# Attention and mixture of experts on one core: the gate's logits from fp16 halves in three products

## The chip, the core and the metric

The kernel runs on one core of a Trainium2 chip. Its time is device time in microseconds (us). Engines: PE (TensorE, matmuls and transposes; its weight loads are listed as PEld), DVE (VectorE), ACT (ScalarE), POOL (GpSimd), and SP, which only issues DMAs here. PE writes to PSUM, a small memory of 8 banks that DVE and ACT read. Each engine runs its instructions in the order of the program and waits where an operand is not there yet.

## The reference

Three stages: attention in a causal window of 128 keys, a mixture of experts with one expert per token, and a dense layer with the maximum of three products. The change touches the gate's logits, between the first and the second.

```python
def _attn_ref(q, k, v):                       # q, k, v: [4, 8, 576, 64]
    ...
    return np.matmul(attn, v)

def _moe_ref(x, modality_id, w_gate, modality_bias, w1, w2):   # x: [2304, 512], 8 experts
    logits = x @ w_gate + modality_bias[modality_id]
    e_idx = np.argmax(logits, axis=1)
    ...                                        # probs = softmax(logits)
    gate_w = probs[np.arange(N), e_idx]
    for e in range(E):
        mask = e_idx == e
        h = np.maximum(x[mask] @ w1[e], 0.0)
        out[mask] = gate_w[mask, None] * (h @ w2[e])

def _moe2_ref(x, w1, w2, w3, w_out):
    h = np.maximum(np.maximum(x @ w1, x @ w2), x @ w3)
    return h @ w_out
```

## The kernel before

Tokens are taken in tiles of 128 rows of one batch entry b: tiles t = 0 to 3 are full, t = 4 has 64 rows. A group is (b, t, g) with g = 0 or 1 for four of the eight heads; t = 4 holds all heads in one group. `run` (L485) walks over 36 groups and issues, in group n, work of several groups: the product with V of group n-3 (`pv`, L390, on PE), the softmax of group n (four score reductions L348 on DVE, four exponentials L357 on ACT), the scores of group n+1 or n+2 (`qk`, L335), the transposes of group n-1's exponentials (L376) with their split into an fp16 high half (ACT, L382) and low half (DVE, L387), and the normalisation (L432 to L436 on DVE). Where a product has to be more precise than fp16, both operands are held as a high and a low fp16 half and three products are added: high by high, high by low, low by high (PASSES, L916).

When both head groups of a tile are done, its rows are turned by `xt` (L453): four transposes on PE into a PSUM tile (L458), and a copy to SBUF in fp32 on ACT (L460). `logits` (L463) is issued one group later: four fp32 matmuls of 128x8 against the gate weights wg (L468). `logit_out` (L478) adds the modality's bias on DVE (L479) and writes to L, from which `Route` finds each token's expert. The last full tile (t = 3) and the half tile (t = 4) of a batch entry come in the same group; there the first one's logits are issued directly behind its transposes.

The first groups run alone (from the start to about 97 us). Then `att.mixed` is set, and the attention's steps are woven between the matmuls of the experts' first batches (`slot`, L978; products L994 and L1015, weights split by L957 on ACT and L966 on DVE). In this mode the logits are issued at the start of a group, right behind `qk`, and their output follows at once. Which step stands where is fixed when the program is built. Four PSUM tiles of the pool psM are shared by transposes, turned rows, logits and the experts' products; one is taken again when its last reader is done. After the attention (about 262 us) DVE converts the third stage's weights (L1110 to L1121).

`RouterConsts.bias` (L172) runs in the first groups as small pieces, one at each call of `fill`, between the reductions of the softmax.

Of the kernel before, what the change touches and what calls it, by code (L numbers as in the profile page):

```python
# [7 lines left out]
F32 = mybir.dt.float32  # L8
F16 = mybir.dt.float16
BF16 = mybir.dt.bfloat16  # L10
I32 = mybir.dt.int32
ACTF = mybir.ActivationFunctionType
ALU = mybir.AluOpType
# [4 lines left out]
E, FF, F2 = 8, 1024, 768  # L18
WIN = 128
HALF = NT // 2  # L20
NTB = 5
# [10 lines left out]
KD, KF, K2 = DM // 128, FF // 128, F2 // 128  # L32
SV = 256.0
SX = 64.0
SW = 64.0
# [6 lines left out]
NG = 2  # L42
WAIT = 3
PLACES = 2


@with_exitstack
def windowed_attention_moe_kernel(
# [16 lines left out]
    nc = tc.nc  # L65
    PSUM = bass.MemoryType.PSUM
    const = ctx.enter_context(tc.tile_pool(name="const", bufs=1))
# [16 lines left out]
    iota_e = const.tile([128, 2 * NTB, E], F32, name="iota_e")  # L84
    ones_r = const.tile([1, 128], F16, name="ones_r")
    wg = const.tile([128, KD, E], F32, name="wg")
    mbt = const.tile([128, B, NTB, E], F32, name="mbt")
    parts = const.tile([128, 2 * NTB, 6], F16, name="parts")

# [21 lines left out]
    class Bias:  # L111


        def __init__(self, pool, pf, bias, nq, widths):
            self.bias, self.nq = bias, nq
            tot = sum(widths)
            self.rf = pf
            if nq < 128:
                self.rf = pool.tile([128, 1], F32, name=f"c_rf{nq}")
                nc.vector.tensor_copy(self.rf[0:nq], pf[0:nq])  # L120
                nc.vector.tensor_scalar(self.rf[nq:], pf[nq:], float(-nq), None, ALU.add)
            self.ci = pool.tile([128, tot], I32, name=f"c_ci{nq}")
            o = 0
            for w, base in zip(widths, (-WIN, 0)):
                nc.gpsimd.iota(
                    self.ci[:, o:o + w], base=base,
                    pattern=[[1, w]], channel_multiplier=0,
                )
                o += w
            self.rel = pool.tile([128, tot], F32, name=f"c_rel{nq}")  # L130
            self.t = pool.tile([128, tot], F32, name=f"c_t{nq}")
# [23 lines left out]
    class RouterConsts:  # L155
# [16 lines left out]
        def bias(self):  # L172
            pool = self.pool
            mr = pool.tile([36, 128], F32, name="c_mr")
            nc.vector.tensor_copy(
                mr, self.mi.rearrange("r (p two) -> r p two", two=2)[:, :, 0]
            )
            yield 4
            ps = psM.tile([128, 512], F32, name="m", tag="m")
            nc.tensor.transpose(ps[:, 0:36], mr, ident[0:36, 0:36])  # L180
            yield 4
            mf = pool.tile([128, B, NTB], F32, name="c_mf")
            nc.vector.tensor_copy(
                mf[:, :, 0:4], ps[:, 0:16].rearrange("p (b r) -> p b r", r=4)
            )
            nc.vector.tensor_copy(mf[:, :, 4], ps[:, 32:36])
            yield
            mf = mf.rearrange("p b t -> p (b t)")
            mn = pool.tile([128, B * NTB], F32, name="c_mn")
            nc.vector.tensor_scalar(mn, mf, -1.0, 1.0, ALU.mult, ALU.add)  # L190
            yield
            mt = pool.tile([128, B * NTB, E], F32, name="c_mt")
            sh = [128, B * NTB, E]
            mbo = mbt.rearrange("p b t e -> p (b t) e")
            nc.vector.tensor_tensor(
                out=mbo, in0=mn.unsqueeze(2).to_broadcast(sh),
                in1=self.mb[:, 0:1, :].to_broadcast(sh), op=ALU.mult,
            )
            yield
            nc.vector.tensor_tensor(  # L200
                out=mt, in0=mf.unsqueeze(2).to_broadcast(sh),
                in1=self.mb[:, 1:2, :].to_broadcast(sh), op=ALU.mult,
            )
            yield
            nc.vector.tensor_tensor(out=mbo, in0=mbo, in1=mt, op=ALU.add)
# [12 lines left out]
    L = [rt.tile([128, 2 * NTB, E], F32, name=f"L{h}") for h in range(2)]  # L218
# [33 lines left out]
    class Attention:  # L252
# [200 lines left out]
        def xt(self, t, x):  # L453
            kd = KD if t < 4 else KD // 2
            ps = psM.tile([128, KD, 128], F32, name="m", tag="m")
            xf = x.rearrange("p a b c -> p (a b c)")
            for kk in range(kd):
                nc.tensor.transpose(ps[:, kk, :], xf[:, 128 * kk:128 * kk + 128], ident)  # L458
            xt = self.p.tile([128, KD, 128], F32, name="xt", tag="xt", bufs=1)
            nc.scalar.activation(out=xt[:, 0:kd], in_=ps[:, 0:kd], func=ACTF.Copy)  # L460
            return xt

        def logits(self, b, t, xt):  # L463
            ps = psM.tile([128, 512], F32, name="m", tag="m")
            m, kd = (128, KD) if t < 4 else (64, KD // 2)
            for kk in range(KD):
                u, ku = divmod(kk, kd)
                nc.tensor.matmul(  # L468
                    out=ps[0:m, 0:E], lhsT=xt[:, ku, m * u:m * u + m], rhs=wg[:, kk, :],
                    start=(kk == 0), stop=(kk == KD - 1),  # L470
                )
            self.outs.append((b, t, m, ps))

        def logits_out(self):
# [2 lines left out]

        def logit_out(self, b, t, m, ps):  # L478
            nc.vector.scalar_tensor_tensor(  # L479
                out=L[b // 2][0:m, NTB * (b % 2) + t, :], in0=ps[0:m, 0:E], scalar=1.0 / SX,  # L480
                in1=mbt[0:m, b, t, :], op0=ALU.mult, op1=ALU.add,
            )
            self.got.add((b, t))
# [379 lines left out]
    class Gather:  # L863
# [42 lines left out]
        def send(self):  # L906
            for i in range(len(self.out)):
# [4 lines left out]
                    in_=xc[0:o.shape[3]].rearrange("p a c -> p (a c)"),  # L912
                )
                self.sent += 1

    PASSES = ((0, 0), (0, 1), (1, 0))  # L916

    class Weights:

# [58 lines left out]
    def slot(pool, wst, w0, xT, yT, d, cap):  # L978
# [9 lines left out]
        for m in range(KF):  # L988
# [3 lines left out]
            for kk in range(KD):  # L992
                for wl, xl in PASSES:
                    nc.tensor.matmul(  # L994
# [12 lines left out]
        for dm in range(KD):  # L1007
# [3 lines left out]
            for f in range(KF):  # L1011
                if f in (2, 4, 6):
                    yield 6 * cap / 2370, 0.6 if f == 4 and cap > 256 else 0
                for wl, xl in PASSES:
                    nc.tensor.matmul(  # L1015
# [128 lines left out]
    def moe2(pool, items, w, hmt, n2=C2, both=False, **kw):  # L1144
# [5 lines left out]
        def product(run, yT, c, m, i):  # L1150
            ps = psM.tile([128, 512], F32, name="m", tag="m")[:, 0:n2]
            n = 0
            for kk in range(KD):
                for wl, xl in PASSES:
                    nc.tensor.matmul(  # L1155
# [35 lines left out]
        def outer(x, yT, c, idxs, gates):  # L1191
            w.convert(w.n)
            hm = hms[:, x % 2]
            for u in range(n2 // 128):
# [3 lines left out]
                for f in range(K2):  # L1198
                    for wl, xl in PASSES:
                        nc.tensor.matmul(  # L1200
# [64 lines left out]
    class Batch:  # L1265
# [30 lines left out]
        def turn(self, wait=WAIT):  # L1296
# [7 lines left out]
            if not self.todo and not self.age and not self.done:  # L1304
                self.done = True
                if self.u % 2:
                    fill.add(self.r.late())
            for _ in range(PLACES):
                if self.age and self.age[0] >= wait:
# [210 lines left out]
```

## Time and profile before

| what | value |
|---|---|
| median of three runs | 695.49 us (693.38 to 697.06) |
| profiled execution | 695.69 us, span 693.9 us |
| PE busy | 644.1 us (93% of the span) |
| DVE busy | 351.8 us (51%) |
| ACT busy | 346.3 us (50%) |
| POOL busy | 222.5 us (32%) |
| granted clock of PE, mean | 0.979 |

The span runs from the first to the last instruction; the profiled execution's time is 1.8 us longer. Busy shares are means over stages with different limits, so the views by stretch tell more than the page's first section. A row of the timeline gives the start, the time from the start to the end of the last of its instructions, the engine, the line, and in square brackets the idle time ahead of it with what ended it. The end of a matmul is modelled and matmuls overlap, so the cost of small matmuls is read from starts.

### The profile page before, as it was taken

To read this page: it belongs to the slowest core of one execution; us is meant where nothing else is said; L and a number is where in the kernel's file an instruction comes from. 1 tells how busy PE (TensorE), PEld (TensorE's weight loads), DVE (VectorE), ACT (ScalarE), POOL (GpSimd) and SP (SyncE) were. 2 spreads that over 40 slices of the span, in tenths; PEclk is the share of its full clock that TensorE was granted. 3 is DMA by queue.
4 is the path that set the end of the run, shared out by engine and by line. 5 is a ranking of instruction groups with operands and counts; after the bars stand their busy time and mean duration, and the time that the engine had idled before them with its cause. 6 is when DMAs were issued, how large, how long until landed. Compare 5 with 4: busy or idle time off the path is not lost.

```text
span 693.9 us, 12894 instructions
## 1 busy us (share of the span) xinstructions
PE 644.1 (93%) x4787; PEld 401.9 (58%) x4787; DVE 351.8 (51%) x1083; ACT 346.3 (50%) x660; POOL 222.5 (32%) x232
## 2 busy tenths in 40 slices
PE   6899879999898989688899999999999999999993
PEld 4687756566665658354455564444447766656641
DVE  5977853875457656799971233062224455201100
ACT  5898876877777646645552211354647211111110
POOL 2111214524323213556662311482424111121121
PEclk9999988999999999899999999999999999999998
DMA  9655755345522237636833403344230000000011
GB/s 192 108 123 136 198 137 140 92 124 166 152 63 73 80 115 238 218 125 209 212 91 76 92 22 122 110 132 121 92 112 13 1 0 1 1 31 17 0 47 49
DMA packets 120800, 69.95 MB, mean 101 GB/s; under 512 B 68872, under 2 KB 115484, under 8 KB 120732
## 3 DMA queue, kind: packets, MB, share of 16 engines
q1 hardware_dynamic: 116992, 59.06, 32.0%
q0 software_dynamic: 3040, 9.96, 4.4%
q8 instruction: 40, 0.66, 0.4%
q14 instruction: 28, 0.23, 0.1%
q10 hardware_dynamic: 700, 0.04, 0.1%
HBM read 57.19 MB, written 9.44 MB: 96 GB/s over the span
## 4 chain that ended last, share of the span: by engine, by line
PE 71%; DVE 15%; ACT 7%; issue 3%; DMA 3%; POOL 0%; ACTq 0%; POOLq 0%; DVEq 0%
PE m L1155 22%; PE m L1015 12%; PE m L994 11%; PE m L1200 10%; PE s L335 4%; DVE b L1115 3%; PE m L376 3%; PE m L468 2%; PE bank L406 2%; PE m L283 2%; DMA st<-in_moe_w_dram 2%; DVE e L348 2%; DVE b L1121 1%; DVE b L1110 1%; ACT eh L382 1%
## 5 line engine op out<-in xcount | busy, mean ns | idle before, releaser
L1155 PEld LDWEIGHTS <-g 128*128 128x128 f16 x1296 | 128.1, 99 | 100.2 <-issue 12.7
L1155 PE MATMUL m<-yT,g 128*128 128x384 f16 x648 | 111.6, 336 | 11.9 <-ACT hx L1162 4.3
L1155 PE MATMUL m<-yh,g 128*128 128x384 f16 x648 | 105.7, 326 | 0.0
L966 DVE SCALAR_TENSOR_TENSOR wt<-st,wt 128x1024 f16<-128x1024 f32 x48 | 61.6, 1286 | 84.1 <-ACT wt L957 84.1
L1015 PE MATMUL m<-ht,wt 128*128 128x496 f16 (+3 forms) x576 | 101.9, 331 | 1.6 <-DVE wt L966 0.9
L1164 DVE SCALAR_TENSOR_TENSOR hx<-m,hx 128x384 f32<-128x384 f32 x72 | 39.8, 554 | 118.5 <-PE m L1155 117.9
L994 PEld LDWEIGHTS <-wt 128*128 128x128 f16 x576 | 54.6, 98 | 45.1 <-issue 3.2
L986 POOL TENSOR_TENSOR ht<-hf,ht 128x496 f16<-128x496 f32 (+3 forms) x48 | 50.1, 1049 | 86.7 <-ACT ht L985 78.5
L1015 PEld LDWEIGHTS <-wt 128*128 128x128 f16 x576 | 53.8, 98 | 39.3 <-DVE wt L966 1.1
L357 ACT ACTIVATE e<-e,nm 128x256 f32<-128x256 f32 (+2 forms) x144 | 59.8, 472 | 29.1 <-DVE nm L348 27.5
L984 ACT ACTIVATE hf<-m 128x496 f32<-128x496 f32 (+3 forms) x72 | 35.7, 496 | 59.0 <-PE m L1015 36.8
L994 PE MATMUL m<-xT,wt 128*128 128x496 f16 (+2 forms) x288 | 57.7, 341 | 3.1 <-ACT wt L957 1.6
L348 DVE CUSTOM_DVE_ANT_0 e<-s,bias 128x256 f32<-128x256 f32 (+1 forms) x128 | 46.0, 381 | 17.4 <-PE s L335 8.6
L957 ACT ACTIVATE wt<-st 128x1024 f16<-128x1024 f32 x48 | 50.0, 1045 | 4.3 <-DMA st<-in_moe_w_dram 4.2
L994 PE MATMUL m<-xh,wt 128*128 128x496 f16 (+1 forms) x288 | 51.1, 330 | 0.0
L387 DVE TENSOR_TENSOR el<-m,eh 128x512 f16<-128x512 f32 x64 | 42.4, 682 | 11.6 <-ACT eh L382 11.5
L335 PE MATMUL s<-kT,qT 64*128 64x256 f32 (+2 forms) x320 | 42.6, 384 | 3.3 <-DVE nm L348 2.2
L1186 POOL TENSOR_TENSOR xh<-hx,xh 128x384 f16<-128x384 f32 x18 | 16.4, 913 | 89.8 <-ACT xh L1185 89.8
L311 POOL TENSOR_TENSOR vl<-rawv,vh 128x512 f16<-128x512 f32 (+1 forms) x20 | 22.9, 1146 | 68.7 <-ACT vh L304 68.7
L1185 ACT ACTIVATE xh<-hx 128x384 f16<-128x384 f32 x18 | 9.4, 523 | 71.1 <-DVE hx L1164 67.1
L1206 ACT ACTIVATE ob<-m,gate 128x512 f32<-128x512 f32 x18 | 12.4, 687 | 55.0 <-PE m L1200 49.6
L382 ACT ACTIVATE eh<-m 128x512 f16<-128x512 f32 x64 | 34.8, 586 | 7.1 <-PE m L376 6.6
(184 smaller groups left out, 976.5 us busy)
## 6 DMA issues: line engine op xcount, KB each, us to landing
st<-in_moe_w_dram SPq DMA_DIRECT2D x66, 512.0 KB, 4.1
rawk<-in_k_dram SPq DMA_DIRECT2D x16, 256.0 KB, 3.3
rawq<-in_q_dram SPq DMA_DIRECT2D x16, 256.0 KB, 4.1
rawv<-in_v_dram SPq DMA_DIRECT2D x16, 256.0 KB
xs<-x SPq DMA_DIRECT2D x16, 256.0 KB, 2.1
st<-in_moe_w_out_dram SPq DMA_DIRECT2D x6, 512.0 KB, 6.3
rawk<-in_k_dram SPq DMA_DIRECT2D x4, 128.0 KB, 3.4
rawq<-in_q_dram SPq DMA_DIRECT2D x4, 128.0 KB, 4.9
```

The costliest lines, as they stand in the source:

```text
L335: nc.tensor.matmul(out=out[u][rows, x // 2, c0:c1], lhsT=self.qT[b, t][r, i, 0:n], rhs=self.kT[b][r, i, k0 + c0:k0 + c1], start=True, stop ...
L348: nc.vector.tensor_tensor_reduce(out=e[:, x, c0:c1], in0=s[x % 2][:, x // 2, c0:c1], in1=bias[:, x, c0:c1], scale=-0.125, scalar=3.0e38, o ...
L357: nc.scalar.activation(out=e[:, x, c0:c1], in_=e[:, x, c0:c1], func=ACTF.Exp, scale=-1.0, bias=nm[:, x:x + 1],)
L382: nc.scalar.activation(out=b, in_=a, func=ACTF.Copy)
L387: nc.vector.tensor_tensor(out=o, in0=a, in1=b, op=ALU.subtract)
L957: nc.scalar.activation(out=wt[:, 0], in_=st, func=ACTF.Copy, scale=SW)
L966: nc.vector.scalar_tensor_tensor(out=wt[:, 1], in0=st.rearrange("p (a b) -> p a b", a=a), scalar=SW, in1=wt[:, 0], op0=ALU.mult, op1=ALU.s ...
L986: nc.gpsimd.tensor_tensor(out=lo, in0=hf, in1=hi[1], op=ALU.subtract)
L994: nc.tensor.matmul(out=ps, lhsT=wt[:, wl, kk, o:o + 128], rhs=xT[:, xl, kk, bass.ds(d[0], cap)], start=(n == 0), stop=(n == 3 * KD - 1),)
L1015: nc.tensor.matmul(out=ps, lhsT=wt[:, wl, f, :], rhs=hs[f][:, xl], start=(n == 0), stop=(n == 3 * KF - 1),)
L1155: nc.tensor.matmul(out=ps, lhsT=w.g[:, wl, i, m, kk, :], rhs=yT[:, xl, kk, c:c + n2], start=(n == 0), stop=(n == 3 * KD - 1),)
L1200: nc.tensor.matmul(out=ps, lhsT=hm[:, xl, f, 128 * u:128 * u + 128], rhs=w.wo[:, wl, f, :], start=(n == 0), stop=(n == 3 * K2 - 1),)
```

## The change

The turned rows leave PSUM as two fp16 halves: ACT copies the high one, DVE subtracts it from PSUM to get the low one. The tile xt has two buffers instead of one. The gate weights, scaled by SW = 64, are split once into a high and a low half (wgs), in two new pieces of `RouterConsts.bias`. The logits become three fp16 matmuls for each of the four parts of the row, twelve in all, and the output divides by SW too.

```diff
+PASSES = ((0, 0), (0, 1), (1, 0))
...
+    wgs = const.tile([128, KD, 2, E], F16, name="wgs")
...
+            yield
+            nc.vector.tensor_scalar(wgs[:, :, 0], wg, SW, None, ALU.mult)
+            yield
+            nc.vector.scalar_tensor_tensor(
+                out=wgs[:, :, 1], in0=wg, scalar=SW, in1=wgs[:, :, 0],
+                op0=ALU.mult, op1=ALU.subtract,
+            )
             yield 4
...
-            xt = self.p.tile([128, KD, 128], F32, name="xt", tag="xt", bufs=1)
-            nc.scalar.activation(out=xt[:, 0:kd], in_=ps[:, 0:kd], func=ACTF.Copy)
+            xt = self.p.tile([128, 2, KD, 128], F16, name="xt", tag="xt", bufs=2)
+            nc.scalar.activation(out=xt[:, 0, 0:kd], in_=ps[:, 0:kd], func=ACTF.Copy)
+            nc.vector.tensor_tensor(
+                out=xt[:, 1, 0:kd], in0=ps[:, 0:kd], in1=xt[:, 0, 0:kd], op=ALU.subtract
+            )
...
-                nc.tensor.matmul(
-                    out=ps[0:m, 0:E], lhsT=xt[:, ku, m * u:m * u + m], rhs=wg[:, kk, :],
-                    start=(kk == 0), stop=(kk == KD - 1),
-                )
+                for i, (wl, xl) in enumerate(PASSES):
+                    nc.tensor.matmul(
+                        out=ps[0:m, 0:E], lhsT=xt[:, xl, ku, m * u:m * u + m],
+                        rhs=wgs[:, kk, wl, :],
+                        start=(kk == i == 0), stop=(kk == KD - 1 and i == 2),
+                    )
...
-                out=L[b // 2][0:m, NTB * (b % 2) + t, :], in0=ps[0:m, 0:E], scalar=1.0 / SX,
+                out=L[b // 2][0:m, NTB * (b % 2) + t, :], in0=ps[0:m, 0:E], scalar=1.0 / (SX * SW),
```

## Rows read from the trace of the kernel before

**Rows 1.** Stretches: length, then busy PE, PEld, DVE, ACT, POOL; clock, DMA.
```profile
20.00:34.00 14.00, 11.45 (x101) 8.14 (x100) 13.60 (x57) 12.14 (x27) 2.38 (x4) 1.00 0.54 103
...
34.00:97.00 63.00, 57.65 (x741) 49.61 (x742) 45.44 (x216) 52.94 (x120) 13.45 (x19) 0.97 0.63 157
104.00:262.00 158.00, 150.86 (x1427) 99.61 (x1427) 95.67 (x350) 110.45 (x210) 51.69 (x51) 0.99 0.39 111
262.00:360.00 98.00, 82.50 (x565) 53.14 (x565) 86.90 (x151) 51.70 (x98) 57.26 (x49) 0.93 0.62 191
```

**Rows 2.** Chain of waits, 34 to 97 us: start, length, engine, tile, line.
```profile
36.48 0.99 PE m L468 x8
...
95.08 0.99 PE m L468 x8
```

**Rows 3.** Line L468: durations least, median, greatest; starts; forms.
```profile
L468 PE MATMUL m<-wg,xt x160: 172/256/277, 36.4 to 261.8; 128*128 128x8 f32 x128, 128*64 128x8 f32 x32
```

**Rows 4.** Timeline of PE around a full tile's logits and a half one's.
```profile
157.40 1.06 PE L468 MATMUL m<-wg,xt 128*128 128x8 f32 x8
158.31 0.19 PE L406 MATMUL bank<-vh,eh 128*128 128x65 f16 x1
...
159.00 0.19 PE L406 MATMUL bank<-vh,el 128*128 128x65 f16 x1
...
61.27 0.63 PE L468 MATMUL m<-wg,xt 128*64 128x8 f32 x8
61.83 0.87 PE L376 MATMUL m<-ident,e 128*128 128x128 f32 x6
```

**Rows 5.** Timeline of PE, the routing's small products.
```profile
67.58 0.24 PE L662 MATMUL bank<-r_oh,ones 128*128 128x32 bf16 x4
67.68 0.28 PE L666 MATMUL bank<-r_gt,ones 128*128 128x40 bf16 x5
```

**Rows 6.** Lines L387 and L898, the subtraction of an fp16 half from PSUM.
```profile
L387 DVE TENSOR_TENSOR el<-m,eh x64: 667/681/692, 18.6 to 246.6; 128x512 f16<-128x512 f32 x60, 64x512 f16<-64x512 f32 x4
...
L898 DVE TENSOR_TENSOR xT<-m,xT x10: 416/681/692, 98.2 to 184.7; 128x512 f16<-128x512 f32 x8, 128x448 f16<-128x448 f32 x1, 128x256 f16<-128x256 f32 x1
```

**Rows 7.** Timeline around the turned rows copied at 43.18 us.
```profile
41.76 0.35 DVE L348 CUSTOM_DVE_ANT_0 e<-s,biast 128x192 f32<-128x192 f32 x1
...
43.18 0.59 ACT L460 ACTIVATE xt<-m 128x512 f32<-128x512 f32 x1
...
43.32 0.16 DVE L432 TENSOR_SCALAR rd<-bank 128x4 f32<-128x4 f32 x1 [0.65 <-PE bank L406]
...
44.22 1.28 DVE L387 TENSOR_TENSOR el<-m,eh 128x512 f16<-128x512 f32 x2
...
45.49 1.09 PE L376 MATMUL m<-ident,e 128*128 128x128 f32 x8 [0.58 <-ACT kT L297]
```

**Rows 8.** Timeline around the turned rows copied at 71.12 us.
```profile
70.39 0.40 DVE L348 CUSTOM_DVE_ANT_0 e<-s,bias 128x256 f32<-128x256 f32 x1
...
71.12 0.59 ACT L460 ACTIVATE xt<-m 128x512 f32<-128x512 f32 x1
...
73.18 0.16 DVE L432 TENSOR_SCALAR rd<-bank 128x4 f32<-128x4 f32 x1 [0.88 <-PE bank L406]
...
78.22 0.16 PE L786 MATMUL bank<-r_e,ones_r 1*128 1x1 f16 x1 [0.93 <-DVE rd L432]
```

**Rows 9.** Timeline of the woven stretch: one copy, and two logit outputs.
```profile
138.43 0.58 ACT L460 ACTIVATE xt<-m 128x512 f32<-128x512 f32 x1
...
141.95 0.17 DVE L479 SCALAR_TENSOR_TENSOR L<-m,mbt 128x8 f32<-128x8 f32 x1 [3.54 <-PE m L468]
...
248.85 0.17 DVE L479 SCALAR_TENSOR_TENSOR L<-m,mbt 128x8 f32<-128x8 f32 x1 [0.40 <-PE m L468]
```

**Rows 10.** Timeline around a batch entry's last full tile, near 190 us.
```profile
190.15 0.69 DVE L387 TENSOR_TENSOR el<-m,eh 128x512 f16<-128x512 f32 x1 [1.69 <-ACT eh L382]
...
190.66 1.06 PE L468 MATMUL m<-wg,xt 128*128 128x8 f32 x8 [0.93 <-ACT xt L460]
```

More of the change, by code (lines that the diff above doesn't have):

```diff
@@ L914, in send @@
                 self.sent += 1
-    PASSES = ((0, 0), (0, 1), (1, 0))
     class Weights:
```

## The prediction

> **What bounds the kernel now.** I read the stretches first. From 104 to 262 us, where MoE products are woven into the attention, PE is busy 150.86 of 158 us and DVE 95.67: PE is the bound and DVE has room. From 34 to 97 us, where attention runs alone, PE is busy 57.65 of 63 us, ACT 52.94 and DVE 45.44: three engines take turns, each waiting for another. From 262 to 360 us DVE is busy 86.90 of 98 us with work that the change does not touch [rows 1]. The order of instructions on every engine is fixed in the program, so time won or lost before 262 us moves all that follows by the same amount; I count only there. The chain of waits says the same of the first stretch: of its eight logit tiles, five are on the chain, from the one at 36.48 to the one at 95.08 [rows 2]. For the other three something else ends later.
>
> **What is removed.** A logit tile is four fp32 products, recorded as eight matmuls; there are 16 full tiles and 4 half ones [rows 3]. A full one holds PE from its start at 157.40 to the next work at 158.31, 0.91 us; a half one from 61.27 to 61.83, 0.56 us [rows 4]. The change puts twelve fp16 matmuls of 8 columns there. No row shows these, so I bound them: 24 fp16 matmuls with 128x128 weights and 65 columns start between 158.31 and 159.00, 30 ns apart [rows 4]; four with 16-bit weights and 8 to 32 columns start between 67.58 and 67.68, 25 ns apart [rows 5]. Twelve cost 0.30 to 0.36 us; I take 0.33, since 8 columns are nearest to the second row. PE saves 0.58 us in a full tile and 0.23 in a half one: 16 x 0.58 + 4 x 0.23 = 10.2 us if all of it lay on the path.
>
> The Trainium skill, page "FP8 and Floating Point Precision", section "TensorE Precision Notes", speaks against so large a saving: it counts true fp32 as four passes through the array, so that four fp32 products are 16 passes against twelve now. By that a full tile would still take 12/16 of its time. The rows show 25 to 30 ns for one 16-bit matmul and 114 ns (0.91/8) for one of the fp32 records, so here a pass of fp32 is not the price of a small fp16 matmul; but the rule is kept as a rival.
>
> **What is added.** DVE subtracts the fp16 half from PSUM, once per tile. The same operation on 128x512 takes 0.68 us (L387) and on 128x256 0.42 us (L898) [rows 6]: 16 x 0.68 + 4 x 0.42 = 12.6 us of DVE. ACT's copy keeps its shape and place; as fp16 output I cost it as before. The second buffer of the turned rows gives nothing: no row shows a copy that waits for the logits before it. The two conversions of the gate weights fall where DVE is busy 13.60 of 14 us [rows 1]; at 0.16 us for a tiny DVE operation [rows 7] that is +0.3.
>
> What matters is where the subtraction stands. DVE runs in program order. In the first stretch the subtraction is issued behind group n's work and ahead of the four score reductions of group n+1, and it waits for ACT's copy, which waits for PE's transposes. Three of these reductions now run early, while DVE would otherwise wait for the product with V. Take the tile at 43.18. ACT's copy ends at 43.77, the subtraction at 44.49; the three reductions that now run from 41.76 follow it (0.28 us apart) to 45.32. L432, now at 43.32, comes at 45.32, and the two L387, 0.9 us behind it and now at 44.22, come at 46.2. These release the PSUM that PE's next transposes need: the second half of what starts at 45.49 waits until 46.9 instead of about 46.0, and so does all behind it [rows 7]. Loss +1.1, and the 0.58 that PE saved is waited away. At 71.12 the same happens: the copy ends at 71.71, the subtraction at 72.4, 1.9 us of DVE work begun at 70.39 goes behind it, and L432 moves from 73.18 to about 74.3; PE waits for DVE there already (0.93 us at 78.22) [rows 8]. Loss +1.2. The other six tiles of the stretch I worked the same way; where DVE's wait for PE is over 2 us, the shift vanishes: +0.2, 0, +0.3 (full and half tile together), +0.5 and -0.6 (there the whole saving arrives). The subtraction also releases the PSUM of the transposes, later than ACT did, and the next transposes of K wait for that; this is in these numbers. Sum of the first stretch +2.7, bounds -2.9 (all five tiles on the chain save 0.58 and nothing waits) and +9.7 (seven full tiles each pay 0.59 + 0.68 and the half one 0.80).
>
> In the second stretch DVE sits idle 3.54 us ahead of the logit output at 141.95, because it waits for PE's logits. ACT's copy at 138.43 ends at 139.0, so the subtraction ends at 139.7, before the logits start at about 140.9: it is hidden there [rows 9]. Five full tiles are like that: 5 x 0.58 = -2.9. The three half tiles save 3 x 0.23 = -0.7. One tile (output at 248.85) has only 0.40 us of that idle time, and routing work ahead of the subtraction on DVE [rows 9]: +0.2. At the last full tile of a batch the logits are issued right behind the transposes and wait already, 0.93 us at 190.66; DVE is in L387 until 190.84, so the subtraction ends at 191.52 and the rest of the twelve at 191.8 instead of 191.57 [rows 10]. Three such tiles: +0.3, +0.1, +0.1. Behind the subtraction on DVE is the low half of a MoE weight, up to 2.6 us later; it is made two weight tiles ahead, and PE is hardly idle in this stretch, so I cost that at nothing (if that lead were gone, some 1 us a time). Sum -2.9; bounds -5.9 (all nine full tiles save the whole 0.58) and 0 (each saving is waited away).
>
> **Sum.** +0.3 + 2.7 - 2.9 = +0.1 us. The profiled execution took 695.69 us; its span is 693.9, and the 1.8 around it stay. 695.69 + 0.1 = 695.8; it lies 0.2 above the median of the runs, so I forecast 695.6.
>
> **Rivals.** *Faster*: the first stretch has slack that my step by step shift overstates; then the five tiles on the chain give 0.58 each. -2.9 - 2.9 + 0.3 = -5.5, 690 us. For it: DVE has 17.6 us of idle time there [rows 1]. Against: that idle time lies ahead of L432, and the two places worked above have 0.65 and 0.88 us of it, less than copy and subtraction together, 1.27.
> *Slower*: the wait of DVE for ACT's copy is paid in full by every tile of the first stretch, since DVE, PE and ACT each wait for the other in a ring. +9.7 - 2.9 + 0.3 = +7.1, 702.6 us. It decides wherever the idle time ahead of L432 is under 1.27 us and the late PSUM release reaches PE. For it: the two places. Against: the places with over 2 us of slack.
> *The products cost more*, a mechanism of their own: a tile takes 0.91 x 12/16 = 0.68 instead of 0.33. Five tiles lose 0.35, one of the first stretch too, three half tiles 0.09: +2.4, 698 us. It is the fp32 rule named above; the rows of 25 to 30 ns speak against it.
>
> **Chances.** Forecast 0.45, faster 0.28, slower 0.23, dear products 0.04. The forecast's own range is 692 to 699. For eight times in ten I reach into both sides: 689.5 to 701. About 0.5% (3.5 us, 692.0 to 699.0) is what a measurement of this kernel can tell from no change. Faster by more: 0.28 and a little of the forecast's edge, 0.30. Slower by more: 0.23 and an edge, 0.25. Within: 0.45.
>
> **What would show it.** After the change: the logit matmuls 25 to 30 ns apart; the subtraction 0.68 us, with DVE idle ahead of it for ACT's copy; in the first stretch L432 and L387 later against the group's start, and PE waiting for L387 or for the subtraction; in the second stretch the wait of the logit output shorter by some 0.6, PE's busy time 5 to 6 us less, and its end (262 us) within 2 us of where it is. I am wrong if the stretch 34 to 97 gets shorter (then DVE's order did not matter), if PE waits for MoE weights from DVE, or if the granted clock falls at new places.

## The result, and the profile after

The changed kernel takes 700.04 us (median, 698.55 to 703.26) against 695.08 us before (693.38 to 697.06) in the same comparison: a ratio of 1.008, 95% interval 1.006 to 1.010. It is slower by 5 us. That lies inside the range (689.5 to 701.0), above the forecast's own range (692 to 699), 4.4 us above the forecast and on the side that had a chance of 0.25. The profiled execution of after has a span of 699.2 us, 5.3 us over that of before.

The stretches of after, cut as in [rows 1] (length, then busy PE, PEld, DVE, ACT, POOL; clock, DMA):

```profile
20.00:34.00 14.00, 11.85 (x99) 8.73 (x98) 12.48 (x51) 11.75 (x25) 2.39 (x4) 0.92 0.49 97
34.00:97.00 63.00, 54.18 (x714) 44.30 (x714) 46.93 (x213) 50.63 (x112) 12.36 (x18) 0.93 0.60 146
104.00:262.00 158.00, 147.21 (x1445) 93.30 (x1445) 106.00 (x367) 112.45 (x211) 51.62 (x50) 0.98 0.39 108
262.00:360.00 98.00, 82.90 (x578) 53.87 (x579) 83.16 (x148) 52.21 (x99) 53.66 (x46) 0.91 0.61 188
```

From 34 to 97 us PE is busy 3.5 us less than in [rows 1] with 27 matmuls fewer: less work was done in the same time, and the mean granted clock fell from 0.97 to 0.93. From 104 to 262 us PE is busy 3.7 us less and DVE 10.3 us more.

The logit products and the subtraction are what the steps said. Line L481 (L468 before) and the timeline of PE:

```profile
L481 PE MATMUL m<-wgs,xt x240: 166/166/217, 38.7 to 267.3; 128*128 128x8 f16 x96, 128*64 128x8 f16 x24
...
38.73 0.46 PE L481 MATMUL m<-wgs,xt 128*128 128x8 f16 x12
...
39.04 1.08 PE L385 MATMUL m<-ident,e 128*128 128x128 f32 x8
```

The next work starts 0.31 us behind the first of the twelve (0.33 forecast; 0.91 before [rows 4]). What surrounds them is not. Here is the tile that the prediction worked through [rows 7], now copied at 44.91 us (start, length, engine, line, tile; in brackets the idle time before it and what ended it):

```profile
44.91 0.58 ACT L469 ACTIVATE xt<-m 128x512 f16<-128x512 f32 x1
44.93 0.48 PE L344 MATMUL s<-kT,qT 64*128 64x128 f32 x2
...
45.53 0.69 DVE L470 TENSOR_TENSOR xt<-m,xt 128x512 f16<-128x512 f32 x1 [1.97 <-ACT xt L469]
...
46.14 0.35 DVE L357 CUSTOM_DVE_ANT_0 e<-s,biast 128x192 f32<-128x192 f32 x1
...
46.92 0.68 PE L344 MATMUL s<-kT,qT 64*128 64x128 f32 x6 [1.51 <-DVE nm L357]
```

DVE stands still for 1.97 us until ACT has copied, subtracts, and only then makes the score reductions (L357). PE stops 1.51 us in the middle of the next score products: their PSUM tile has three buffers, and the readers that free one are those reductions. This link, from the subtraction to PE by way of the scores, was not in the prediction. DVE's own order came out as worked: L441 starts 2.06 us behind the start of the copy (46.97), where the prediction had 2.14. The chain of waits of after, 34 to 97 us, runs straight through it:

```profile
43.96 1.06 ACT eh L391 x2
45.02 0.49 ACT xt L469
45.53 0.69 DVE xt L470
```

DVE's wait for the copy recurs at nearly every tile. Waits of 34 to 97 us (total us, times, longest): first three rows of after, then the row of before that they replace.

```profile
DVE xt L470 <- ACT xt L469: 8.5, 7, 2.0
...
DVE rd L441 <- PE bank L415: 2.6, 2, 1.4
...
PE s L344 <- DVE nm L357: 1.7, 2, 1.5
```
```profile
DVE rd L432 <- PE bank L406: 8.3, 7, 2.2
```

DVE's idle time ahead of L432 (now L441) shrank from 8.3 to 2.6 us: it was the slack that should have hidden the subtraction, and 8.5 us of waiting for the copy took its place. What this costs PE is counted further below.

The last full tile of a batch entry, where the logits are issued right behind the transposes (before: [rows 10]):

```profile
190.56 1.38 PE L1006 MATMUL m<-xT,wt 128*128 128x480 f16 x6
...
193.33 0.18 PE L481 MATMUL m<-wgs,xt 128*128 128x8 f16 x1 [0.95 <-ACT xt L469]
...
193.57 0.68 DVE L470 TENSOR_TENSOR xt<-m,xt 128x512 f16<-128x512 f32 x1
...
194.31 0.43 PE L481 MATMUL m<-wgs,xt 128*128 128x8 f16 x11 [0.81 <-DVE xt L470]
...
194.86 2.00 PE L1006 MATMUL m<-xT,wt 128*128 128x480 f16 x6
...
197.50 2.07 PE L1006 MATMUL m<-xT,wt 128*128 128x480 f16 x6
...
195.00:200.00 5.00, 5.00 (x21) 2.69 (x20) 1.56 (x2) 3.37 (x8) 1.10 (x1) 0.66 0.25 74
```

The first product waits 0.95 us for the copy as before, the eleven others 0.81 us for the subtraction. Behind this the granted clock of 195 to 200 us is 0.66, a time spent mostly at the lower of its two levels, and six MoE products that take 1.38 us ahead of it take 2.00 and 2.07 behind it.

How far the work stood, by the start of ACT's copy of the turned rows, in five profiled executions (mixedonly, firstlate3 and firstpool are explained below):

| copy of | before | after | mixedonly | firstlate3 | firstpool |
|---|---|---|---|---|---|
| 2nd tile | 43.18 | 44.91 | 42.49 | 42.76 | 40.30 |
| 3rd | 50.27 | 54.23 | 49.57 | 50.75 | 47.40 |
| 5th full | 71.12 | 75.67 | 70.40 | 71.36 | 66.24 |
| 6th | 80.93 | 86.49 | 80.22 | 84.41 | 79.51 |
| 7th | 91.79 | 97.79 | 87.96 | 94.89 | 91.64 |
| 8th | 110.34 | 114.36 | 103.21 | 111.84 | 110.66 |
| 12th | 190.02 | 192.68 | 181.49 | 191.81 | 187.48 |
| 16th | 258.33 | 262.34 | 249.44 | 260.12 | 253.65 |

After is 6.0 us late at the 7th tile, 4.0 at the 8th, 2.7 at the 12th and 4.0 at the 16th. Not all of this is the change. The 1.7 us at the 2nd tile come with a mean granted clock of 0.78 between the first copy and the second; firstonly, which runs the same instructions up to 97 us, has 1.00 there and its 2nd copy at 42.56 us. And before itself is slow from the 6th copy to the 8th: 29.41 us, where mixedonly, which leaves these tiles as they were, takes 22.99 (more under "What stays open"). From the 8th to the 12th copy the hidden tiles of the woven stretch give back 1.4 us.

### The profile page after: what moved, and what is told of

The parts are those of the page before. It is cut to its first block, busy times and chain, and to the rows that moved or that the text cites. A ratio compares the mean times of both kernels' runs of the same rounds, so it can differ in the third digit from the quotient of the medians.

```text
span 699.2 us, 13066 instructions
## 1 busy us (share of the span) xinstructions
PE 644.0 (92%) x4867; PEld 397.6 (57%) x4867; DVE 362.8 (52%) x1105; ACT 348.4 (50%) x660; POOL 223.8 (32%) x232
## 4 chain that ended last, share of the span: by engine, by line
PE 69%; DVE 15%; ACT 7%; DMA 4%; issue 3%; SPq 0%; POOL 0%; ACTq 0%; POOLq 0%; DVEq 0%
PE m L1167 24%; PE m L1006 12%; PE m L1027 12%; PE m L1212 8%; PE s L344 4%; PE m L385 3%; DVE b L1127 2%; PE m L292 2%; DVE e L357 2%; PE bank L415 2%; DMA st<-in_moe_w_dram 2%; DMA out_dram<-ob,tidx 2%; DVE el L396 1%; ACT eh L391 1%; DVE b L1133 1%
## 5 line engine op out<-in xcount | busy, mean ns | idle before, releaser
L1006 PE MATMUL m<-xT,wt 128*128 128x496 f16 (+2 forms) x288 | 59.4, 347 | 3.3 <-ACT wt L969 1.6
L357 DVE CUSTOM_DVE_ANT_0 e<-s,bias 128x256 f32<-128x256 f32 (+1 forms) x128 | 46.0, 381 | 16.1 <-PE s L344 8.6
L344 PE MATMUL s<-kT,qT 64*128 64x256 f32 (+2 forms) x320 | 45.2, 390 | 5.7 <-DVE nm L357 3.9
L396 DVE TENSOR_TENSOR el<-m,eh 128x512 f16<-128x512 f32 x64 | 42.4, 682 | 10.3 <-ACT eh L391 10.2
```

The source lines that it names most:

```text
L344: nc.tensor.matmul(out=out[u][rows, x // 2, c0:c1], lhsT=self.qT[b, t][r, i, 0:n], rhs=self.kT[b][r, i, k0 + c0:k0 + c1], start=True, stop ...
L357: nc.vector.tensor_tensor_reduce(out=e[:, x, c0:c1], in0=s[x % 2][:, x // 2, c0:c1], in1=bias[:, x, c0:c1], scale=-0.125, scalar=3.0e38, o ...
L396: nc.vector.tensor_tensor(out=o, in0=a, in1=b, op=ALU.subtract)
L1006: nc.tensor.matmul(out=ps, lhsT=wt[:, wl, kk, o:o + 128], rhs=xT[:, xl, kk, bass.ds(d[0], cap)], start=(n == 0), stop=(n == 3 * KD - 1),)
```

## The experiments

Ratios are against the kernel before, run beside it on the same chip, and each is given with its 95% interval; 0.1% is 0.7 us. The median of before was 691.8 us beside nosub, subonly, mixedonly and firstonly, 691.6 beside nosub2, late, latelist and mixedlist, 695.8 beside firstlate3, late3 and late3list, and 694.1 beside firstpool, so the ratios are to be compared and not the times.

**nosub.** The change without the subtraction, each high half used in its place.

```diff
-            nc.vector.tensor_tensor(
-                out=xt[:, 1, 0:kd], in0=ps[:, 0:kd], in1=xt[:, 0, 0:kd], op=ALU.subtract
-            )
...
-                        out=ps[0:m, 0:E], lhsT=xt[:, xl, ku, m * u:m * u + m],
+                        out=ps[0:m, 0:E], lhsT=xt[:, 0, ku, m * u:m * u + m],
```

> The changed kernel without DVE's subtraction: the second of the three products takes the high half of the rows again, so PE runs the same twelve matmuls and only the low half's part of the logits is missing. Theory (the subtraction's place in DVE's order is the loss): the saving on PE arrives; five tiles of the first stretch and nine of the second give 0.58 us each and three half tiles 0.23, so about 695 - 8.8 = 686 to 690 us. Rival (the twelve matmuls or the conversions of the gate weights cost it, or PE's clock falls because PE has less to do): it stays near the changed kernel, 697 to 700 us.

842.66 us, ratio 1.219 (1.216 to 1.222). The high half was multiplied twice, so the logits about doubled and tokens went to other experts: the trace has 64 splits of an expert's weight tile where before has 48, and the loop for left-over tokens ran. This tells nothing of the question; nosub2 below replaces it.

**subonly.** The kernel before, with the subtraction added and its result unused.

```diff
+            xl = self.p.tile([128, KD, 128], F16, name="xl", tag="xl", bufs=2)
+            nc.vector.tensor_tensor(
+                out=xl[:, 0:kd], in0=ps[:, 0:kd], in1=xt[:, 0:kd], op=ALU.subtract
+            )
```

> The kernel before with an extra subtraction of the same size from PSUM on DVE, right behind the copy of the turned rows, whose result nobody reads; logits stay fp32. Theory (order on DVE): the first stretch pays the wait in front of the next group's reductions and nothing is saved, some +6 us there, nothing in the second stretch: 700 to 703 us. Rival (DVE has room for 12.6 us of subtractions; the loss is elsewhere): 695 to 696 us.

699.12 us, ratio 1.0107 (1.0086 to 1.0128). The subtraction costs 7.4 us even where no product waits for it. From the 8th copy of turned rows to the 16th the profile is as long as before's (148.10 against 147.99 us), so the loss comes with the tiles of the first stretch, as expected. Whether the place in DVE's queue or the amount of work makes it, this run does not tell; the runs from late on change the place.

**nosub2.** The change without the subtraction; the product that needs the low half runs against zero weights, so that PE's work is that of the change.

```diff
-                        out=ps[0:m, 0:E], lhsT=xt[:, xl, ku, m * u:m * u + m],
-                        rhs=wgs[:, kk, wl, :],
+                        out=ps[0:m, 0:E], lhsT=xt[:, 0, ku, m * u:m * u + m],
+                        rhs=wgs[:, kk, wl, :] if not xl else wgz[:, kk, :],
```

> The changed kernel without DVE's subtraction; the product of the rows' low half is replaced by one of the high half with a weight block of zeros, so PE runs the same twelve matmuls and the low half's part of the logits (some 1e-4 of them) is left out. Theory (the subtraction's place in DVE's order is the loss): the whole saving on PE shows, up to 8.8 us: ratio to the kernel before 0.985 to 0.993. Rival (the twelve matmuls are dear, or PE's clock falls because PE has less to do): ratio 1.003 to 1.01, as with the subtraction.

682.01 us, ratio 0.9855 (0.9836 to 0.9874): 10.1 us faster. The shorter products bring about the whole 10.2 us that 20 tiles save on paper, and "products dear" falls. Between this and the change lies only the subtraction: 1.008 - 0.9855 = 2.25%, 15.6 us, for 12.6 us of DVE work. That is also more than the 7.4 us of subonly. A part is the granted clock: its mean is 0.981 over the five runs of nosub2 and 0.970 over the seven of the change, which by an estimate (difference times 690 us) is 7 to 8 us. That the products themselves now wait for the low half, which they do not in subonly, is the likely rest; it was not measured apart.

**mixedonly** and **firstonly.** The split in the woven stretch alone, and in the first stretch alone; the other tiles keep the fp32 copy and products. The edit of mixedonly (firstonly has the opposite condition):

```diff
+            if not (self.mixed):
+                xt = self.p.tile([128, KD, 128], F32, name="xf", tag="xf", bufs=1)
+                nc.scalar.activation(out=xt[:, 0:kd], in_=ps[:, 0:kd], func=ACTF.Copy)
+                return xt, False
```

> fp16 halves and three products only for the tiles turned in the second stretch, where the experts' products are woven in; the first stretch as before. Theory: the first stretch ends as before, the second gives back between 0.2 us (as the changed kernel's trace has it) and 2.9 us (as forecast): 692 to 695 us. Rival (the second stretch loses too): above 696 us.

> fp16 halves and three products only for the tiles turned in the first stretch, where attention runs alone; the second as before. Theory: the loss is here, +4 us at the start of the experts' products, so 698 to 700 us. Rival: the loss is in the second stretch or behind it, and this is 694 to 696 us.

mixedonly: 688.97 us, ratio 0.9965 (0.9944 to 0.9985), -2.4 us. firstonly: 699.79 us, ratio 1.0096 (1.0068 to 1.0123), +6.7 us. The two add up to the change within their intervals. The loss comes with the tiles of the first stretch; the woven one gains nearly what was forecast.

**late** and **latelist.** The whole change, with the subtraction of the first stretch issued behind the next group's reductions and low halves, and the logits a group later. latelist also leaves the logits of a batch entry's last full tile to the following group, instead of forcing them behind the transposes.

```diff
-            nc.vector.tensor_tensor(
-                out=xt[:, 1, 0:kd], in0=ps[:, 0:kd], in1=xt[:, 0, 0:kd], op=ALU.subtract
-            )
+            self.subs.append((xt[:, 1, 0:kd], ps[:, 0:kd], xt[:, 0, 0:kd]))
...
                 if n - 2 in ehl:
                     self.low(ehl[n - 2])
+                self.sub()
...
-                    if n + 1 in lgs:
-                        self.logits(*lgs.pop(n + 1))
-                    lgs[n + 1] = (b, t, self.xt(t, x))
+                    self.sub()
+                    lgs.setdefault(n + (1 if self.mixed else 2), []).append((b, t, self.xt(t, x)))
```

> The changed kernel with the subtraction of the first stretch moved: behind the next group's score reductions and behind the low halves of the exponentials, and the logits one group later; the second stretch as in the change. Same work. Theory (order on DVE): the wait in front of the reductions is gone, some 5 of the 6.6 us that the split costs when it is made in the first stretch alone come back, ratio 0.990 to 1.000. Rival (12.6 us more work on DVE in a ring of three engines cost that, wherever it stands; or the transposes' PSUM that is held longer costs as much): 1.005 to 1.012.

> As the run with the late subtraction, and the last full tile of a batch entry does not have its logits issued right behind its transposes any more but with the half tile's, one group later, in both stretches. Theory: PE's waits there (0.95 for ACT and 0.8 us for DVE, three or four times) vanish: 3 to 6 us below the run with the late subtraction, ratio 0.984 to 0.994. Rival (other engines end last at these places): no difference to that run.

late: 692.92 us, ratio 1.0026 (1.0009 to 1.0043). latelist: 689.74 us, 0.9975 (0.9961 to 0.9988). Late misses its 0.990 to 1.000, and latelist its 0.984 to 0.994. Late's trace shows a side effect: with logits and routing later, more of the attention runs alone before the MoE products begin (its 8th tile is copied at 98.34 us and its first MoE product starts at 105.2; in after they stand at 114.36 and 106.5), so the places compared are not the same ones. That the forced logits cost 0.5% stands, since the two kernels share all else.

**mixedlist.** mixedonly, without the forced logits in the woven stretch.

> fp16 halves only for the tiles of the second stretch (0.9965 of the kernel before when run alone), and there the last full tile's logits one group later. Theory: three waits of 1.7 us and what PE's clock loses behind them vanish, another 3 to 6 us: ratio 0.988 to 0.993. Rival: 0.996 as without the later logits.

683.26 us, ratio 0.9891 (0.9869 to 0.9912): 7.5 us faster than the kernel before, and the fastest that computes all of the reference. Its trace at the place of the forced logits:

```profile
183.02 1.38 PE L1020 MATMUL m<-xT,wt 128*128 128x480 f16 x6
185.39 0.93 PE L493 MATMUL m<-wgs,xt 128*128 128x8 f16 x24
187.53 2.59 PE L1020 MATMUL m<-xT,wt 128*128 128x480 f16 x12
```

Full and half tile go together, nothing waits ahead of them, and the MoE products keep 1.38 us for six behind them. Against mixedonly this is worth 0.74%, 5.1 us.

**firstlate3, late3 and late3list.** The order alone: the subtraction behind the reductions and low halves, as in late, but the logits still in the same group, behind the transposes of the probabilities. firstlate3 splits the first stretch only, late3 all tiles; late3list also leaves the forced logits to the next group.

```diff
                     self.high(ehl[n - 1])
+                for a in lgs.pop(n, ()):
+                    self.logits(*a)
+                self.logits_out()
```

> Halves and three products only for the tiles of the first stretch, as in the run that was 1.0096 of the kernel before, but there the subtraction stands behind the next group's score reductions and low halves, and the logits still come in that next group, behind its transposes. Same work on every engine as in that run, and no logit comes a group later. Theory (order on DVE, not the amount): most of the 6.6 us come back, ratio 0.994 to 1.002. Rival (the amount of DVE's work in a ring of three engines): 1.006 to 1.010.

> The whole change with the same order: subtraction of the first stretch behind the next group's reductions and low halves, logits behind the next group's transposes; the woven stretch as in the change, with the batch entry's last full tile still issued at once. Theory: the first stretch as in the run with the first stretch alone, the second as in the run with the second alone (0.9965): ratio 0.990 to 0.998. If the first late subtraction (1.0026) lost by moving one group of attention out of the woven stretch, this one is 3 to 6 us faster than that; rival: equal to it.

> As that, and the logits of a batch entry's last full tile come with the half tile's one group later. Theory: another 5 us, as between the two runs of the second stretch alone (0.9965 and 0.9891): ratio 0.982 to 0.991, the fastest form with all twelve products. Rival: no faster than the second stretch alone, 0.989 or above.

firstlate3: 702.54 us, ratio 1.0100 (1.0068 to 1.0132). late3: 699.31 us, 1.0055 (1.0029 to 1.0081). late3list: 690.87 us, 0.9932 (0.9908 to 0.9956). All three miss what was expected of them (0.994 to 1.002, 0.990 to 0.998, 0.982 to 0.991). The theory that the order alone makes the loss of the first stretch has fallen: firstlate3 is no faster than firstonly. Its trace says how. Up to the 5th full tile it holds before's pace (71.36 against 71.12 us in the table, where after has lost 4.5 us), so moving the subtraction and the logits did cure those places; late3 and late3list take the same time from the 2nd to the 5th copy (28.59 us each, firstlate3 28.60, before 27.94, firstonly 33.28). Then, at the 6th tile, first firstlate3 and behind it the same work of before:

```profile
76.20 0.80 DVE L741 TENSOR_TENSOR r_op<-iota_r,r_pq 128x640 f16<-128x640 f16 x1
...
77.17 0.67 DVE L480 TENSOR_TENSOR xt<-m,xt 128x512 f16<-128x512 f32 x1
...
77.90 0.43 PE L496 MATMUL m<-wgs,xt 128*128 128x8 f16 x11 [1.41 <-DVE xt L480]
...
80.27 0.16 PE L820 MATMUL bank<-r_e,ones_r 1*128 1x1 f16 x1 [0.72 <-DVE rd L441]
80.36 1.57 PE L344 MATMUL s<-kT,qT 64*64 64x192 f32 x16
...
82.02 1.86 PE L385 MATMUL m<-ident,e 128*128 128x128 f32 x8
...
80.00:84.00 4.00, 3.73 (x33) 2.97 (x33) 2.35 (x10) 1.78 (x5) 0.00 (x0) 0.57 0.98 308
```
```profile
78.31 0.89 PE L335 MATMUL s<-kT,qT 64*64 64x192 f32 x16
...
79.28 1.07 PE L376 MATMUL m<-ident,e 128*128 128x128 f32 x8
```

The subtraction now stands behind the small operations of the routing (L741 and those behind it), the products wait 1.41 us for it, and the granted clock of 80 to 84 us is 0.57: the score products take 1.57 instead of 0.89 us, the transposes 1.86 instead of 1.07. Between the two, PE also waits 0.72 us for DVE (at 80.27). The 1.41 us and the two slower groups together are 2.9 us, nearly all of the 3.2 us lost between the 5th and the 6th copy, and late3 and late3list lose about as much there. The pair late3 and late3list puts the forced logits at 1.2%, the largest of the three measures of them.

**firstpool.** late3list, but in the first stretch ACT copies to fp32 as before the change, and GpSimd makes both halves from that copy in SBUF; DVE has no part in it.

```diff
+            if not self.mixed:
+                xc = self.p.tile([128, KD, 128], F32, name="xc", tag="xc", bufs=2)
+                nc.scalar.activation(out=xc[:, 0:kd], in_=ps[:, 0:kd], func=ACTF.Copy)
+                nc.gpsimd.tensor_copy(xt[:, 0, 0:kd], xc[:, 0:kd])
+                nc.gpsimd.tensor_tensor(
+                    out=xt[:, 1, 0:kd], in0=xc[:, 0:kd], in1=xt[:, 0, 0:kd], op=ALU.subtract
+                )
+                return xt
```

> As late3list, but in the first stretch (34 to 97 us) VectorE has no part in the split: ScalarE copies the turned rows to SBUF in fp32, as before the change, and GpSimd, which did 6 us of work in 34 to 72 us, makes the high half from that copy and then the low half by a subtraction. The woven stretch keeps the subtraction on VectorE, as in mixedlist. Theory (the first stretch loses because the logit products wait for a subtraction that stands in VectorE's queue with the routing's small operations, and because the clock falls behind that wait): the copies of the turned rows up to 100 us stand within 0.6 us of before, the logit products there wait less than 0.5 us in all, and the ratio is 0.979 to 0.988, below mixedlist's 0.9891 by the 0.58 us that each full tile's products save. Rival (a second pass over the tile costs the first stretch whichever engine makes it, because the logits and with them the routing come later): the ratio is 0.992 or above, as for late3list (0.9932).

688.95 us, ratio 0.9922 (0.9902 to 0.9942): the rival's number. On the 5th full tile it is 4.9 us ahead of before (2.0 of them already at the first copy, 31.40 against 33.39 us, ahead of any logits), on the 7th level with it (against mixedonly, which has no slow place there, 3.7 us late). The timeline of PE in between:

```profile
71.72 0.44 PE L492 MATMUL m<-wgs,xt 128*128 128x8 f16 x12 [1.36 <-DVE el L396]
...
74.86 0.16 PE L814 MATMUL bank<-r_e,ones_r 1*128 1x1 f16 x1 [1.03 <-DVE rd L441]
74.94 1.57 PE L344 MATMUL s<-kT,qT 64*64 64x192 f32 x16
...
76.61 1.95 PE L385 MATMUL m<-ident,e 128*128 128x128 f32 x8
...
90.89 0.66 PE L467 MATMUL m<-ident,x 128*128 128x128 f32 x4 [2.54 <-DVE el L396]
```

The products wait 0.2 us in all for a half, but they need a PSUM buffer that DVE frees with the low halves of the probabilities (L396), and DVE is late with those. Again PE stands still, here 1.36 us and, at 74.86, another 1.03 for DVE, and again score products and transposes run at about half the rate behind it (1.57 and 1.95 us). The place of the logits behind the transposes, which the kernel shares with late3list and not with mixedlist, may be a part of this; it was not measured.

## Why the prediction was 4.4 us low

**Products: right.** 0.31 us a tile against 0.33, and nosub2 realises 10.1 of 10.2 us. The Trainium skill's rule of four passes for fp32 ("FP8 and Floating Point Precision", section "TensorE Precision Notes") would have made a tile 0.68 us here; the trace disagrees.

**Subtraction on DVE: right in duration** (0.69 and 0.42 us), and right that DVE idles ahead of it for the copy.

**Second stretch: right within its interval**, as a sum. Forecast -2.9, mixedonly -2.4 us (-3.9 to -1.0). The hidden tiles gave their saving: from copy to copy mixedonly's lead over before grows by 0.58 to 0.61 us at four of the five, and by 0.22 at the other. The tile whose output stood at 248.85 us lost 0.58 (0.2 forecast). The last full tiles had been put at +0.5 together, wait included; in mixedonly, with a mean granted clock of 1.00 in this stretch, two of them cost 0.2 and 0.5 us. In after the place near 193 us cost 2.0 us (its lag grows from 2.7 us at the 12th copy to 4.6 at the 13th), for there the clock fell behind the wait, and the clock was not in the working. Leaving those logits to the next group is worth 3.5 to 8.5 us (0.5, 0.74 and 1.2% in three pairs), though that removes the wait of before [rows 10] as well.

**First stretch: the term that was mis-sized.** Forecast +2.7 (and +0.3 for the weights), measured +6.7 us (4.7 to 8.5) in firstonly. The mechanism was named, DVE waits for the copy and its queue moves back, but its price held waits alone. The time from one copy of turned rows to the next, in brackets the mean granted clock where it is under 1.00 (after and firstonly run the same instructions here):

| full tiles | mixedonly | after | firstonly | nosub2 |
|---|---|---|---|---|
| 1st to 2nd | 9.80 | 11.40 (0.78) | 9.48 | 9.20 |
| 2nd to 3rd | 7.08 | 9.32 (0.82) | 9.07 (0.81) | 7.09 |
| 3rd to 4th | 7.21 | 7.40 | 7.42 | 6.61 |
| 4th to 5th | 13.62 | 14.04 | 16.79 (0.80) | 12.97 |
| 5th to 6th | 9.82 | 10.82 | 10.82 | 9.82 |
| 6th to 7th | 7.74 | 11.30 (0.94) | 8.20 | 7.74 |
| 7th to 8th | 15.25 | 16.57 (0.83) | 16.27 (0.90) | 17.03 (0.80) |

Where the clock stays at 1.00 the steps are about what the prediction worked out: the 5th to the 6th tile takes 1.0 us more (forecast +1.2), the 3rd to the 4th 0.2. Behind the tile worked at 43.18 (forecast +1.1) the loss is 2.0 to 2.2 us; by an estimate (length times one minus the mean granted clock) 1.7 us of it are PE at its lower level, behind the wait of 1.51 us shown above. Subonly has the same there (9.70 us, 0.82); before, mixedonly, mixedlist and nosub2, without a subtraction there, have 7.08 or 7.09 us and 1.00. Over all seven steps firstonly is 7.5 us longer than mixedonly, and the same estimate puts 6.7 on the clock. Runs without a profile say so in part: the mean granted clock is 0.972 over the six runs of firstonly and 0.978 over the 13 of before beside them, by the same estimate some 4 of the 6.7 us. What that leaves, 2.7 us, is near the 3.0 forecast. So the mis-sized term is the clock, put at nothing in the sum and worth half of this loss or more by these estimates. The rule that the shift vanishes where DVE idles over 2 us was incomplete too, for the reductions can hold up PE itself by way of the three score buffers, but at full clock this cost little (0.2 us from the 3rd tile to the 4th, where the scores' weight loads waited 0.37 us for a reduction). The slower rival, every tile paying its wait in full, put the stretch at +9.7; the total lies about halfway, but the steps of 0.2 and 0.4 us are not its mechanism. The cure up to 71 us in firstlate3 shows that the place of subtraction and logits started the losses up to there.

**The granted clock: named as what would make me wrong, and left out of the sum.** After has PE as busy as before, 644.0 against 644.1 us on the two pages, although its products are 10 us shorter: the saving went, at least in part, into matmuls at the lower clock. The sign "PE's busy time 5 to 6 us less" was set for the woven stretch and came out at -3.7 from 104 to 262 us; the end of that stretch is not within 2 us but 4.3 us later (last copy at 264.72 against 260.39). That the time still fell inside the stated range is owed to its reach into the slower rival, not to the sum.

**Behind 262 us.** Forecast 0; the profiled executions differ by 1.0 us more at the end (5.3) than at the last copy (4.3). firstonly and firstlate3 lose some 3 us there, with a granted clock of 0.60 and 0.63 in 258 to 270 us where before has 1.00. Why it falls there is not settled.

**What stays open.** One profiled execution is a poor witness for 3 us. In before, PE sits idle twice for nothing that the profile shows, and the low clock follows; in mixedonly, whose instructions up to 97 us are the same but for the two small conversions of the gate weights, it does not, at nearly the same DMA share (1.08 against 1.05; timeline of PE and slices, before, then mixedonly):

```profile
88.18 0.27 PE L376 MATMUL m<-ident,e 128*64 128x128 f32 x1 [0.20 <-issue]
88.90 0.51 PE L376 MATMUL m<-ident,e 128*64 128x128 f32 x3 [0.45 <-issue]
...
84.00:88.00 4.00, 3.98 (x51) 3.46 (x51) 1.73 (x9) 3.06 (x8) 3.09 (x4) 1.00 1.10 298
88.00:92.00 4.00, 2.13 (x11) 1.61 (x11) 2.71 (x13) 1.75 (x5) 1.29 (x4) 0.83 1.05 310
```
```profile
86.24 1.09 PE L385 MATMUL m<-ident,e 128*128 128x128 f32 x8
87.27 0.66 PE L467 MATMUL m<-ident,x 128*128 128x128 f32 x4
...
88.00:92.00 4.00, 4.00 (x52) 3.56 (x53) 2.62 (x14) 3.53 (x10) 1.71 (x3) 1.00 1.08 321
```

From the 6th to the 7th copy before takes 10.86 us, mixedonly 7.74, and from the 7th to the 8th 18.55 (clock 0.75) against 15.25. So 6.4 us of mixedonly's lead in the table are no work of the change, its span (685.2) is 8.7 us shorter than before's where the ratio makes 2.4, and the same slow place of before hides as much of after's lag in that table. Whether this idle time is in most executions of before cannot be told from one profile each. Nor is it settled which falls of the clock the change brings about: those from the 1st to the 2nd copy of after and from the 4th to the 5th of firstonly are each in only one of two profiles of the same instructions. Open too is whether any place in the first stretch makes the split pay: in three orders and on two engines it did not, and PE waited at another place where the traces were read.

## What to carry to other kernels

An operation added to an engine that serves two others in a ring is not hidden just because that engine idles further down its queue: ask which buffers are freed by what now stands behind it, and who needs them, before asking how long it takes. Where a tight stretch and one with slack share a helper, change the one with slack alone: here the split in the woven stretch, with its logits a group later so that nothing waits for the subtraction, gives -1.1%, while the whole change gives +0.8%. And price a new wait of TensorE together with the matmuls behind it: here the waits were worked out nearly right, and the clock behind them made most of the miss, by the estimates above.

## What was not expected of the hardware

At three places, waits of TensorE were followed by matmuls at about half the rate: 2.00 to 2.07 for 1.38 us behind the 0.95 and 0.81 us of waits at 193 us in after, 1.57 for 0.89 and 1.86 for 1.07 behind 1.41 and 0.72 us in firstlate3, 1.57 and 1.95 for the same groups behind 1.36 and 1.03 us in firstpool. Each time the slower groups shown cost 1.3 to 1.6 us more. Behind the single 0.93 us waits of before at 190.66 [rows 10] and 78.22 [rows 8] the same work kept its rate, but also behind two waits of 0.73 and 1.03 us in after (at 80.64 and 83.78) and of 1.58 and 0.67 us in mixedonly (at 96.41 and 97.67), with a granted clock of 1.00. Which waits the lower clock follows is not settled by these runs. GpSimd subtracts a 128x512 tile from SBUF in 1.16 us, where DVE takes 0.69 from PSUM; its conversion of the tile takes 0.61.
